# Way back of a Fourier-mix and SoLU kernel: PSUM columns side by side, output tiles by n2 runs, r formed on GpSimd, new schedule keys

## The chip, the cores and the metric

The kernel runs on one core of one Trainium2 chip. The metric is device time in microseconds from launch to end, as the median of several runs. A profiled execution of the same kernel gives the trace that is read below.

## The reference

For each of 8 batches a real Fourier transform along the sequence (3136 positions, 256 channels), a complex 256 x 256 matrix product with bias, a soft threshold, and the inverse transform; then, for each of the 25088 resulting rows, a feed-forward layer with 1024 hidden units, SoLU and a layer norm:

```python
X = np.fft.rfft(x, axis=1)
Yr = Xr @ w_r - Xi @ w_i + b_r
Yi = Xr @ w_i + Xi @ w_r + b_i
Yr = np.sign(Yr) * np.maximum(np.abs(Yr) - lam, 0.0)      # and Yi alike
y = np.fft.irfft(Y, n=3136, axis=1)                       # rows of the second part
h = y @ w_in
e = np.exp(h - h_max)
solu = h * e / (np.sum(e) + 1e-09)
ln = (solu - mu) / np.sqrt(var + 1e-06) * g_ln
out = ln @ w_out
```

All inputs and the output are float32; w_in and w_out come as wide words that the kernel narrows itself.

## The kernel before

The sequence of 3136 is split as 98 x 32 (n1 x n2), so each transform is two small ones. On the way there, `fwd1` transforms along n1 (matmuls with `fq_s` or `fa_s`), `fwd2` along n2 (with `fb`), `mix` multiplies by the weights (`w_hi`, `w_lo`), `threshold` follows on GpSimd, and on the way back `inv1` goes along n2 (with `gb`) and `inv2` along n1 (with `ia_s`, or `iaf_s` in float32 for batch 0). Most factors are split into two f16 parts, high and low, so a product takes three matmuls. Between the steps the data go through DRAM (`s1`, `s2`).

`inv2(b, g)` takes a group of `G2` = 4 values of n2: it loads `zt`, and for each half `eh` of the channels runs 4 x 3 matmuls of 98 columns into one PSUM bank `pv`, seen as (n1, i) with i one of the 4 values of n2. ScalarE then rounds the bank to f16 (`ring_hi`), VectorE forms the rest (`ring_lo`). Of the 98 values of n1 the first 96 go to the rings, the last 2 to `last_hi` and `last_lo`. The rings hold rows of the second part in the order in which they lie there, 128 to a tile.

Each tile of 128 rows goes through three steps. `moe_head`: 12 matmuls of 512 columns with `win_hi`, `win_lo`, `win_low` into a pair of banks, the maximum `m`, some scalars (`ch`, `a`), the exponential on ScalarE and the product `u` on VectorE. `moe_turn`: `lh` (ScalarE) and `ll` (GpSimd), two DMA transposes to `th` and `tl`, the variance `var`, and the scale `r`, in three instructions: a product and sum on VectorE, a power and a product on GpSimd. `moe_tail`: 24 matmuls with `wout`, the scaling by `r` into `o` on ScalarE, and the store of `o`:

```python
out_v = out.rearrange("(b n1 n2) e -> b n1 n2 e", b=B, n1=N1)
n1, n2 = t * P // G2 % N96, t * P // (G2 * N96) * G2
nc.sync.dma_start(out_v[b, n1 : n1 + P // G2, n2 : n2 + G2], o)
```

Every DMA but the first four loads is issued by the one queue of SyncE (SP), in program order. The order of all engines is made at build time by `Plan`: each instruction or group has a key (tables `KEYS`, `SHIFT`, `ROLE`, by stage and role), a cost from `weigh`, and waits; at each point an engine takes the startable operation with the lowest key. All instructions are issued from one line, `issue` (L455, after the change L457), so every row of the profile has that line, and the names of tiles tell the steps apart.

Of the kernel before, what the change touches and what calls it, by code (L numbers as in the profile page):

```python
# [17 lines left out]
AF = mybir.ActivationFunctionType  # L18
ALU = mybir.AluOpType
# [5 lines left out]
S, N1, N2 = 3136, 98, 32  # L25
# [7 lines left out]
S_SCALE, B_SCALE, Z_SCALE, X_SCALE = 2.0**-7, 2.0**-5, 2.0**-11, 2.0**-11  # L33

LOW = 2.0**11
# [209 lines left out]
class Banks:  # L245
# [38 lines left out]


KEYS = {
    "fa": -300, "bias": -182.62, "start": 0, "warm": -200, "plain": -200, "weights": -173.3, "consts": -100,
    "groups": 0, "x0": -51.8, "y0": -216.47, "b0": -80.78, "b0s": 5.87, "w_in0": -120.86, "w_in1": -81.06,
    "w_in": -58.58, "w_out0": -50.76, "w_out": -33.85, "mix": 155.45, "pads": -36.23, "a1": -69.9, "a1s": 8.066,
    "a2": 14.01, "a2s": 1.704, "a": 4.95, "b1": -17.06, "b1s": 1.283, "b": 3.84, "bs": 1.407, "inv2": -93.08,  # L290
    "turn": 239.13, "tail": 4.12, "as": 2.844,
}

SHIFT = {
    "a5": 0.49, "b3": -0.7, "b6": -0.86, "b4": -1.48, "a4": 2.88, "b2": 2.98, "b5": -3.61, "a3": 4.37, "a7": 4.4,
    "a1": -4.81, "a2": -8.16, "a6": -8.71, "b1": 22.31, "b0": -73.49,
}

ROLE = {
    "tail/po": 0.08, "head/u": 0.13, "w_in1/lh": -0.14, "head/ph": -0.28, "tail/o": 0.96, "b/bin": -1.92,  # L300
    "a/bias_y": -2.32, "a/pf": -2.48, "w_out0/lh": 2.64, "w_in1/junk": -2.96, "b/yl": 3.08, "w_out/th": -3.25,
    "b/zs": -3.39, "a/xw0": -3.57, "w_in1/ll": 3.61, "a/un": -4.21, "head/m": -4.36, "inv2/ring_lo": 4.46,
    "w_in1/Du": -5.32, "b/pf": -5.67, "b/Dbin": -5.91, "b/yt": 6.31, "a/hsb": -6.98, "b/y": -8.09,
    "turn/r": -8.25, "b/bin_s16": -8.58, "b/Xh16": -9.67, "w_in0/u": 10.09, "b/Xs": -10.27, "turn/lh": -13.86,
    "a/top": 15.51, "w_out/tl": -15.85, "head/a": 22.29, "tail/Dout": 23.17, "b/Dgb2": 23.89, "a/sc": -25.79,
    "b/zout": -38.98,
}


# [29 lines left out]
class Plan:  # L339
# [68 lines left out]
    def weigh(self, op, name, args, kw, ins, outs):  # L408
        if name == "dma_start":
            v = next(v for v in (*outs, *ins) if not isinstance(v, DramView))  # L410
            size = (v.rows[1] - v.rows[0]) * v.cells.size * mybir.dt.size(v.dtype)
            cross = kw.get("transpose", False)
            op.length += 1600.0 if cross else 430.0
            op.moved += 1500.0 if cross else size / 270.0
        elif op.engine == "tensor":
            moving = ins[-1]
            n = moving.cells.size * (4 if moving.dtype == F32 else 1) * 0.42 + 1
            if moving.cells.size == N1:
                n += 3 * (4 if moving.dtype == F32 else 1)
            lhs = ins[0].tile.kw["name"]  # L420
            op.half = 8 if "gb" in lhs else 4 if lhs == "fq_s" else 2 if moving.tile.kw["name"][:2] == "fb" else 0
            op.length += self.PACE * n / max(op.half, 1)
        else:
            big = max((v.cells.size for v in (*ins, *outs)), default=1)
            scalars = sum(v.cells.size == 1 for v in ins)
            if big == 1:
                scalars -= 2 if name == "tensor_tensor" else 1
            each = self.ELEMENT[op.engine]
            wide = [v for v in ins if v.cells.size > 1]
            sbuf = not any(v.tile.kind.banks for v in (*ins, *outs))  # L430
            if op.engine == "scalar" and sbuf:
                each = 0.87
            if op.engine == "gpsimd" and len(wide) == 2 and all(v.dtype == F32 for v in (*wide, *outs)):
                each = 2.12
            if op.engine == "vector" and sbuf and name in ("tensor_scalar", "tensor_copy") and big > 1:
                each, op.port = 0.545, True
            if op.engine == "vector" and sbuf and len(wide) == 2:
                op.port = True
            if op.engine == "gpsimd":
                op.port = True  # L440
            op.length += self.CALL[op.engine] + big * each + max(scalars, 0) * self.SCALAR[op.engine]
            if "accum_out" in kw and op.engine == "scalar":
                op.length += 92.0
            if ALU.pow in kw.values() or ALU.pow in args:
                op.length += 420.0
# [119 lines left out]
def fft_mix_solu_kernel(ctx: ExitStack, tc, x, w_r, w_i, b_r, b_i, w_in, w_out, g_ln, fa, fq, none, iaf, fb, fs, gb, gs, ia, out):  # L565
    nc = Plan(tc.nc)
    B, _, D = x.shape
    FF = w_in.shape[1]
    P = 128
# [3 lines left out]
    C1 = 1024  # L573
    NCH = N2 * D // C1
    NPK = 8
    out_v = out.rearrange("(b n1 n2) e -> b n1 n2 e", b=B, n1=N1)

    const = Pool(ctx.enter_context(tc.tile_pool(name="const", bufs=1)), 1)
    dram = Pool(ctx.enter_context(tc.tile_pool(name="dram", bufs=2, space=DRAM)), 2, dram=True)
# [4 lines left out]
    banks = Banks(ctx.enter_context(tc.tile_pool(name="ps", bufs=1, space=PSUM)), 8, pf=5, ph=3, po=2, pb=8)  # L584
# [70 lines left out]
    peaks, scales = {}, {}  # L655
# [158 lines left out]
    Xs, Ys = {}, {}  # L814
# [273 lines left out]
    G2 = 4  # L1088
    N96 = N1 - N1 % 16
    R = 2 * G2 * N96  # L1090
    ring_hi = const.tile([P, ND, R], F16, name="ring_hi")
    ring_lo = const.tile([P, ND, R], F16, name="ring_lo")
    lasts = {}

    def inv2(b, g):
        if b >= PLAIN_Z:
            zt = fp.tile([P, G2, 2, D], F16, name="zt", bufs=2)[:N1]
            nc.sync.dma_start(zt.rearrange("c n t d -> c (n t d)"), s2[b][:, g * G2 * 2 * D : (g + 1) * G2 * 2 * D])
        else:
            zt = fp.tile([P, G2, D], F32, name="zt", bufs=2)[:N1]  # L1100
            nc.sync.dma_start(zt.rearrange("c n d -> c (n d)"), s2[b][:, g * G2 * D : (g + 1) * G2 * D])
        j0 = (b * N2 + g * G2) * N96 % R
        if g == 0 and b % 2 == 0:
            lasts[b // 2] = [fp.tile([P, ND, 2, N1 - N96, N2], F16, name=f"last_{part}", bufs=1) for part in ("hi", "lo")]
        for eh in range(ND):
            pv = banks.tile("pf")[:, : G2 * N1].rearrange("p (n i) -> p n i", n=N1)
            to = [
                (
                    ring[:, eh, j0 : j0 + G2 * N96].rearrange("p (n i) -> p n i", n=N96),
                    last[:, eh, b % 2, :, g * G2 : (g + 1) * G2],  # L1110
                )
                for ring, last in zip((ring_hi, ring_lo), lasts[b // 2])
            ]
            nc.reserve(*to[0], *to[1])
            with nc.together():
                for i in range(G2):
                    es = slice(eh * P, (eh + 1) * P)
                    if b < PLAIN_Z:
                        nc.tensor.matmul(pv[:, :, i], zt[:, i, es], iaf_s, start=True, stop=True)
                        continue  # L1120
                    for k, (t, j) in enumerate(((0, 0), (0, 1), (1, 2))):
                        nc.tensor.matmul(pv[:, :, i], zt[:, i, t, es], ia_s[:, j], start=k == 0, stop=k == 2)
            for hi, lo, ns in zip(*to, (slice(0, N96), slice(N96, N1))):
                nc.scalar.activation(hi, pv[:, ns], AF.Copy, scale=X_SCALE)
                nc.vector.scalar_tensor_tensor(lo, hi, -LOW, pv[:, ns], ALU.mult, ALU.add)


    def h_scale(k):
# [48 lines left out]
    def moe_turn(k, u, total, a):  # L1177

        parts = []
        hi = mp.tile([P, FF], F16, name="lh", bufs=2)  # L1180
        nc.scalar.copy(hi, u)
        lo = mp.tile([P, FF], F16, name="ll", bufs=2)
        nc.gpsimd.tensor_sub(lo, u, hi)
        for part, name in ((hi, "th"), (lo, "tl")):
            t = mp.tile([P, NF, P], F16, name=name, bufs=3)
            nc.sync.dma_start(t, part, transpose=True)
            parts.append(t)
        junk = mp.tile([P, FF], BF16, name="junk", bufs=1)
        var = sp.tile([P, 1], F32, name="var")
        nc.scalar.activation(junk, u, AF.Square, bias=total, scale=-float(FF), accum_out=var)  # L1190
        r = sp.tile([P, 1], F32, name="r", bufs=8)
        nc.vector.scalar_tensor_tensor(r, a, a, var, ALU.mult, ALU.add)
        nc.gpsimd.tensor_tensor(r, r, mhalf, op=ALU.pow)
        nc.gpsimd.tensor_tensor(r, r, unscale, op=ALU.mult)
        return k, parts, r

    def moe_tail(k, parts, r):
        th, tl = parts
        po = banks.tile("po")
        n = 0  # L1200
# [6 lines left out]
        o = mp.tile([P, D], F32, name="o", bufs=2)  # L1207
        nc.scalar.activation(o, po[:, :D], AF.Copy, scale=r)
        b, t = k
        if t is None:  # L1210
            for i in range(2):
                nc.sync.dma_start(out[(b + i) * S - P // 2 : (b + i) * S], o[i * P // 2 : (i + 1) * P // 2])
            return
        n1, n2 = t * P // G2 % N96, t * P // (G2 * N96) * G2
        nc.sync.dma_start(out_v[b, n1 : n1 + P // G2, n2 : n2 + G2], o)

# [206 lines left out]
    for b in range(B):  # L1425
# [8 lines left out]
        groups = 0  # L1434
# [36 lines left out]
```

## Time and profile before

| | |
|---|---|
| Median of 3 runs | 1595.03 us (1593.70 to 1598.29) |
| Profiled execution | 1598.61 us, its span 1596.8 us |
| Granted TensorE clock | 0.989 of full speed in the mean |
| Busy share of the span | PE 97%, DVE 83%, ACT 73%, POOL 64% |
| DMA queue of SP | 523596 packets, 268.93 MB, 77.3% of 16 engines' span |

PE is the matmul engine, PEld its weight loads, DVE VectorE, ACT ScalarE, POOL GpSimd, SP the queue that issues DMAs. The span runs from the first to the last instruction. A matmul's duration includes the time in which it overlaps its neighbours, so the distance between starts tells what one costs. A wait is idle time of an engine, put down to what ended it.

### The profile page before, as it was taken

To read this page: it belongs to the slowest core of one execution; us is meant where nothing else is said; L and a number is where in the kernel's file an instruction comes from. 1 tells how busy PE (TensorE), PEld (TensorE's weight loads), DVE (VectorE), ACT (ScalarE), POOL (GpSimd) and SP (SyncE) were. 2 spreads that over 40 slices of the span, in tenths; PEclk is the share of its full clock that TensorE was granted. 3 is DMA by queue.
4 is the path that set the end of the run, shared out by engine and by line. 5 is a ranking of instruction groups with operands and counts; after the bars stand their busy time and mean duration, and the time that the engine had idled before them with its cause. 6 is when DMAs were issued, how large, how long until landed. Compare 5 with 4: busy or idle time off the path is not lost. (4 is left out here: it accounts for less than half of the span.)

```text
span 1596.8 us, 40552 instructions
## 1 busy us (share of the span) xinstructions
PE 1546.1 (97%) x15471; PEld 1090.9 (68%) x15471; DVE 1333.3 (83%) x2767; ACT 1168.7 (73%) x2134; POOL 1017.7 (64%) x1155
## 2 busy tenths in 40 slices
PE   6979999999999999999999999999999999999998
PEld 3435676677666776776776767677776777777776
DVE  5889888978999888888889898888888887777775
ACT  5768777767768877777777767677776877676675
POOL 0646686667766767577764767557765677754554
PEclk8989999999999999999999999999999999999999
DMA  7788768967699598977999789775777965576666
GB/s 251 214 246 181 185 132 183 216 132 164 153 225 198 119 208 181 215 154 167 181 203 214 158 182 204 158 138 121 170 183 166 206 109 130 121 164 139 133 113 123
DMA packets 524239, 273.12 MB, mean 171 GB/s; under 512 B 423680, under 2 KB 501996, under 8 KB 523984
## 3 DMA queue, kind: packets, MB, share of 16 engines
q1 hardware_dynamic: 523596, 268.93, 77.3%
q8 instruction: 121, 1.98, 0.5%
q10 hardware_dynamic: 448, 1.61, 0.3%
q14 instruction: 74, 0.61, 0.1%
HBM read 84.71 MB, written 82.97 MB: 105 GB/s over the span
## 5 line engine op out<-in xcount | busy, mean ns | idle before, releaser
L455 POOL TENSOR_TENSOR ll<-u,lh 128x1024 f16<-128x1024 f32 x196 | 426.3, 2175 | 213.7 <-ACT lh L455 202.2
L455 PE MATMUL store<-wout,th 128*128 128x256 f16 x3136 | 376.6, 273 | 3.7 <-DVE yt L455 2.5
L455 PEld LDWEIGHTS <-th 128*128 128x128 f16 x3136 | 305.9, 99 | 59.2 <-issue 9.7
L455 ACT ACTIVATE u<-store,m,hsb 128x1024 f32<-128x1024 f32 x192 | 231.7, 1207 | 121.7 <-DVE m L455 113.1
L455 DVE TENSOR_REDUCE m<-store 128x1 f32<-128x1024 f32 x196 | 238.9, 1219 | 90.9 <-PE store L455 90.5
L455 PE MATMUL store<-win_hi,ring_hi 128*128 128x512 f16 x768 | 292.6, 381 | 8.1 <-DVE u L455 7.4
L455 PE MATMUL store<-win_lo,ring_hi 128*128 128x512 f16 x768 | 292.3, 381 | 0.0
L455 PE MATMUL store<-win_low,ring_lo 128*128 128x512 f16 x768 | 291.9, 380 | 0.0
L455 ACT CAST lh<-u 128x1024 f16<-128x1024 f32 x196 | 205.6, 1051 | 117.9 <-DVE u L455 69.4
L455 DVE SCALAR_TENSOR_TENSOR u<-store,ch,u 128x1024 f32<-128x1024 f32 x196 | 250.6, 1279 | 40.1 <-ACT u L455 38.4
L455 PEld LDWEIGHTS <-ring_hi 128*128 128x128 f16 x1536 | 149.2, 98 | 154.5 <-issue 17.1
L455 ACT ACTIVATE junk<-u,su 128x1024 bf16<-128x1024 f32 x196 | 226.6, 1156 | 8.3 <-DVE u L455 8.0
L455 PE MATMUL store<-wout,tl 128*128 128x256 f16 x1568 | 203.9, 273 | 0.0
L455 PEld LDWEIGHTS <-tl 128*128 128x128 f16 x1568 | 151.8, 98 | 30.8 <-issue 7.1
L455 PE MATMUL store<-w_hi,Xh 128*128 128x256 f16 (+1 forms) x584 | 166.5, 285 | 6.1 <-ACT Xh L455 3.4
L455 PE MATMUL store<-w_hi,Xl 128*128 128x256 f16 (+1 forms) x584 | 165.9, 284 | 1.4 <-DVE Xl L455 1.1
L455 PE MATMUL store<-w_lo,Xh 128*128 128x256 f16 (+1 forms) x584 | 165.9, 284 | 0.0
L455 DVE SCALAR_TENSOR_TENSOR r<-a,var 128x1 f32<-128x1 f32 x196 | 129.5, 664 | 31.6 <-ACT junk L455 28.3
L455 POOL TENSOR_TENSOR y<-yt,yc 128x512 f32<-128x512 f32 (+1 forms) x104 | 128.1, 1233 | 30.5 <-ACT yt L455 26.2
L455 PEld LDWEIGHTS <-Xh 128*128 128x128 f16 x1168 | 113.8, 99 | 40.7 <-issue 8.9
L455 PEld LDWEIGHTS <-ring_lo 128*128 128x128 f16 x768 | 75.4, 98 | 91.4 <-issue 1.4
L455 POOL TENSOR_TENSOR r<-r,mhalf 128x1 f32<-128x1 f32 x196 | 110.8, 568 | 39.5 <-DVE r L455 26.3
(178 smaller groups left out, 2593.3 us busy)
## 6 DMA issues: line engine op xcount, KB each, us to landing
out_dram<-o SPq DMA_DIRECT2D x192, 128.0 KB
s<-av SPq DMA_DIRECT2D x48, 512.0 KB
zt<-s SPq DMA_DIRECT2D x56, 392.0 KB
s<-zout SPq DMA_DIRECT2D x42, 512.0 KB
xw<-in_x_dram SPq DMA_DIRECT2D x48, 384.0 KB
bin<-s SPq DMA_DIRECT2D x72, 256.0 KB
s1f<-av SPq DMA_DIRECT2D x10, 392.0 KB
xw<-in_x_dram SPq DMA_DIRECT2D x8, 392.0 KB
```

Of the source, the lines that this page charges most:

```text
L455: getattr(engine, name)(*args, **kw)
```

## The change

Four things change. In `inv2` the bank is seen as (i, n1): each matmul writes 98 neighbouring columns, and the rings get rows in the order n2, n1 within a group. A tile of 128 rows is then one to three runs of n1 at fixed n2 (each run of n2 is 96 long), and `moe_tail` stores one run at a time. In `moe_turn` the first of the three instructions for `r` moves from VectorE to GpSimd, as a `tensor_scalar` with two pointers. The tables of keys are new throughout, and `weigh` has a cost for the new GpSimd form.

```diff
 KEYS = {
-    "fa": -300, "bias": -182.62, "start": 0, "warm": -200, "plain": -200, "weights": -173.3, "consts": -100,
+    "fa": -300, "bias": -243.29, "start": 0, "warm": -200, "plain": -200, "weights": -203.16, "consts": -100,
...
+            if op.engine == "gpsimd" and name == "tensor_scalar":
+                each = 1.15
...
-    out_v = out.rearrange("(b n1 n2) e -> b n1 n2 e", b=B, n1=N1)
+    out_v = out.rearrange("(b n1 n2) e -> b n2 n1 e", b=B, n1=N1)
...
-            pv = banks.tile("pf")[:, : G2 * N1].rearrange("p (n i) -> p n i", n=N1)
+            pv = banks.tile("pf")[:, : G2 * N1].rearrange("p (i n) -> p i n", n=N1)
             to = [
                 (
-                    ring[:, eh, j0 : j0 + G2 * N96].rearrange("p (n i) -> p n i", n=N96),
-                    last[:, eh, b % 2, :, g * G2 : (g + 1) * G2],
+                    ring[:, eh, j0 : j0 + G2 * N96].rearrange("p (i n) -> p i n", n=N96),
+                    last[:, eh, b % 2, :, g * G2 : (g + 1) * G2].rearrange("p n i -> p i n"),
...
-                        nc.tensor.matmul(pv[:, :, i], zt[:, i, es], iaf_s, start=True, stop=True)
+                        nc.tensor.matmul(pv[:, i], zt[:, i, es], iaf_s, start=True, stop=True)
...
-                        nc.tensor.matmul(pv[:, :, i], zt[:, i, t, es], ia_s[:, j], start=k == 0, stop=k == 2)
+                        nc.tensor.matmul(pv[:, i], zt[:, i, t, es], ia_s[:, j], start=k == 0, stop=k == 2)
...
-                nc.scalar.activation(hi, pv[:, ns], AF.Copy, scale=X_SCALE)
-                nc.vector.scalar_tensor_tensor(lo, hi, -LOW, pv[:, ns], ALU.mult, ALU.add)
+                nc.scalar.activation(hi, pv[:, :, ns], AF.Copy, scale=X_SCALE)
+                nc.vector.scalar_tensor_tensor(lo, hi, -LOW, pv[:, :, ns], ALU.mult, ALU.add)
...
-        nc.vector.scalar_tensor_tensor(r, a, a, var, ALU.mult, ALU.add)
+        nc.gpsimd.tensor_scalar(r, a, a, var, ALU.mult, ALU.add)
...
-        n1, n2 = t * P // G2 % N96, t * P // (G2 * N96) * G2
-        nc.sync.dma_start(out_v[b, n1 : n1 + P // G2, n2 : n2 + G2], o)
+        p = 0
+        while p < P:
+            n2, n1 = divmod(t * P + p, N96)
+            n = min(N96 - n1, P - p)
+            nc.sync.dma_start(out_v[b, n2, n1 : n1 + n], o[p : p + n])
+            p += n
```

GpSimd's order in the last stretch, before: the power (`r<-r,mhalf`) and the product (`r<-r,unscale`) of one tile's r, then the next tile's `a` and `ll`.

```order
L455 TENSOR_TENSOR ll<-u,lh 128x1024
L455 TENSOR_TENSOR r<-r,mhalf 128x1
L455 TENSOR_SCALAR a<-se,a 128x1
L455 TENSOR_TENSOR r<-r,unscale 128x1
L455 TENSOR_TENSOR ll<-u,lh 128x1024
```

The same place of the change:

```order
L457 TENSOR_TENSOR ll<-u,lh 128x1024
L457 TENSOR_SCALAR r<-a,var 128x1
L457 TENSOR_TENSOR r<-r,mhalf 128x1
L457 TENSOR_SCALAR a<-se,a 128x1
L457 TENSOR_TENSOR r<-r,unscale 128x1
L457 TENSOR_TENSOR ll<-u,lh 128x1024
```

One instruction has come in ahead of the power; VectorE's order has lost its `r<-a,var` rows, 196 in all.

SP's order in the last stretch, before: for each tile two transposes and, between them, the store of an earlier tile.

```order
L455 DMA_TRANSPOSE th<-lh 128x8x128
L455 DMA out_dram<-o 32x4x256
L455 DMA_TRANSPOSE tl<-ll 128x8x128
L455 DMA_TRANSPOSE th<-lh 128x8x128
L455 DMA out_dram<-o 32x4x256
L455 DMA_TRANSPOSE tl<-ll 128x8x128
```

The same place of the change:

```order
L457 DMA_TRANSPOSE th<-lh 128x8x128
L457 DMA out_dram<-o 32x256
L457 DMA out_dram<-o 96x256
L457 DMA_TRANSPOSE tl<-ll 128x8x128
L457 DMA_TRANSPOSE th<-lh 128x8x128
L457 DMA out_dram<-o 96x256
L457 DMA out_dram<-o 32x256
L457 DMA_TRANSPOSE tl<-ll 128x8x128
```

Every store has become two, of 96 and 32 rows or of 64 and 64, between the same transposes; 200 stores of `o` have become 392.

PE's order at the very start, before (the `fa_s` matmuls are the first transform of batch 0, the `yc` matmuls spread the biases, the `u,ones` ones sum the weights):

```order
L455 MATMUL store<-ones 128x128 x12
L455 MATMUL store<-xw_86,fa_s 98x512 x2
L455 MATMUL store<-u,fa_s 98x512 x2
L455 MATMUL store<-xw_86,fa_s 98x512 x2
L455 MATMUL store<-u,fa_s 98x512 x4
L455 MATMUL store<-xw_100,fa_s 98x512 x2
L455 MATMUL store<-u,fa_s 98x512 x2
L455 MATMUL store<-xw_100,fa_s 98x512 x2
L455 MATMUL store<-yc,ones 128x512
L455 MATMUL store<-yc,yt 128x256 x2
L455 MATMUL store<-u,ones 128x256 x4
```

The same place of the change:

```order
L457 MATMUL store<-ones 128x128 x12
L457 MATMUL store<-xw_86,fa_s 98x512 x2
L457 MATMUL store<-yc,ones 128x512
L457 MATMUL store<-yc,yt 128x256 x2
L457 MATMUL store<-u,fa_s 98x512 x4
L457 MATMUL store<-xw_86,fa_s 98x512 x2
L457 MATMUL store<-u,fa_s 98x512 x2
L457 MATMUL store<-xw_101,fa_s 98x512 x2
L457 MATMUL store<-u,fa_s 98x512 x2
L457 MATMUL store<-xw_101,fa_s 98x512 x2
L457 MATMUL store<-u,ones 128x256 x4
```

The bias matmuls have moved ahead of most of the first transform; PE has 29863 rows in both orders.

## Rows read from the trace of the kernel before

**Rows 1.** The page, busy time, share of the span and instructions of each engine.

```profile
PE 1546.1 (97%) x15471; PEld 1090.9 (68%) x15471; DVE 1333.3 (83%) x2767; ACT 1168.7 (73%) x2134; POOL 1017.7 (64%) x1155
```

**Rows 2.** Busy time by stretch: length, each engine, granted clock, DMA share, GB/s.

```profile
0.00:100.00 100.00, 80.72 (x837) 39.82 (x837) 75.09 (x142) 70.77 (x135) 40.77 (x40) 0.93 0.77 235
...
300.00:1500.00 1200.00, 1186.22 (x12149) 856.15 (x12148) 1018.00 (x2115) 887.10 (x1624) 793.48 (x906) 1.00 0.79 168
```

**Rows 3.** The chain that ended last: start, length, what.

```profile
1213.37 379.10 PE store L455 x3467
```

**Rows 4.** PE's waits: total us, times, longest us (first two, last of 20).

```profile
PE store L455 <- DVE u L455: 7.9, 9, 2.2
PE store L455 <- ACT bin L455: 6.9, 1, 6.9
...
PE store L455 <- POOL Xl L455: 0.2, 1, 0.2
```

**Rows 5.** PE in order of time, 1300 to 1310 us: start, length, what.

```profile
1300.16 1.57 PE L455 MATMUL store<-fb,bin 64*128 64x64 f16 x96
1301.67 1.05 PE L455 MATMUL store<-wout,tl 128*128 128x256 f16 x8
1302.55 0.38 PE L455 MATMUL store<-win_hi,ring_hi 128*128 128x512 f16 x1
...
1305.14 2.19 PE L455 MATMUL store<-ia_s,zt 98*128 98x98 f16 x24
1307.12 1.95 PE L455 MATMUL store<-wout,th 128*128 128x256 f16 x16
1308.91 1.04 PE L455 MATMUL store<-wout,tl 128*128 128x256 f16 x8
1309.79 0.27 PE L455 MATMUL store<-w_hi,Xh 128*128 128x256 f16 x1
```

**Rows 6.** Groups of PE by form: count, busy us, mean ns, idle before.

```profile
L455 PE MATMUL store<-ia_s,zt 98*128 98x98 f16 x1344 | 122.2, 286 | 1.6 <-ACT o L455 0.9 <-DVE yt L455 0.6
...
L455 PE MATMUL store<-iaf_s,zt 98*128 98x98 f32 x128 | 15.3, 274 | 0.0
```

**Rows 7.** PE in order of time, at 111 and at 456 us.

```profile
111.14 3.71 PE L455 MATMUL store<-iaf_s,zt 98*128 98x98 f32 x32
114.68 0.38 PE L455 MATMUL store<-win_hi,ring_hi 128*128 128x512 f16 x1
...
456.25 0.40 PE L455 MATMUL store<-fs_s,bin_s 128*128 128x128 f16 x4
456.48 0.71 PE L455 MATMUL store<-wout,th 128*128 128x256 f16 x5
```

**Rows 8.** Groups of ACT by form.

```profile
L455 ACT ACTIVATE ring_hi<-store 128x384 f16<-128x384 f32 x128 | 62.1, 495 | 40.5 <-PE store L455 40.1
...
L455 ACT ACTIVATE Xh<-store 128x512 f16<-128x512 f32 x104 | 57.2, 603 | 19.3 <-DVE Xs L455 13.9 <-PE store L455 5.1
```

**Rows 9.** Groups of DVE and of POOL by form.

```profile
L455 DVE SCALAR_TENSOR_TENSOR r<-a,var 128x1 f32<-128x1 f32 x196 | 129.5, 664 | 31.6 <-ACT junk L455 28.3 <-POOL r L455 1.1 <-POOL yc L455 1.0
...
L455 POOL TENSOR_SCALAR yc<-yt,sc 128x512 f32<-128x512 f32 x84 | 68.6, 817 | 56.6 <-DVE yt L455 40.0 <-DVE ch L455 15.2 <-DVE a L455 1.1
L455 POOL TENSOR_SCALAR a<-se,a 128x1 f32<-128x1 f32 x196 | 56.1, 286 | 95.9 <-ACT u L455 37.2 <-DVE a L455 33.5 <-PE store L455 2.1
```

**Rows 10.** SP's issues in order of time, 1502 to 1556 us.

```profile
1502.17 1.24 SPq L455 DMA_TRANSPOSE th<-lh  x1
1503.65 0.56 SPq L455 DMA_DIRECT2D out_dram<-o  x1
1504.31 1.27 SPq L455 DMA_TRANSPOSE tl<-ll  x1
...
1555.12 1.23 SPq L455 DMA_TRANSPOSE th<-lh  x1
```

**Rows 11.** Busy time by stretch, columns as in rows 2.

```profile
640.00:680.00 40.00, 40.00 (x384) 28.53 (x382) 34.82 (x92) 30.65 (x57) 20.68 (x29) 1.00 1.07 209
```

More of the change, by code (lines that the diff above doesn't have):

```diff
@@ L286 @@
 KEYS = {
-    "fa": -300, "bias": -182.62, "start": 0, "warm": -200, "plain": -200, "weights": -173.3, "consts": -100,
[L288 to L291, printed above, removed]
+    "fa": -300, "bias": -243.29, "start": 0, "warm": -200, "plain": -200, "weights": -203.16, "consts": -100,
@@ L292 @@
+    "groups": 0, "x0": -175.82, "y0": -51.96, "b0": -115.32, "b0s": 4.277, "w_in0": -161.15, "w_in1": -112.71,
+    "w_in": -109.53, "w_out0": -71.07, "w_out": -17.01, "mix": 116.28, "pads": -69.29, "a1": -75.67,
+    "a1s": 10.825, "a2": 18.06, "a2s": 1.034, "a": 0.49, "b1": -21.98, "b1s": 1.959, "b": 2.06, "bs": 1.538,
+    "inv2": -85.41, "turn": 153.65, "tail": 3.96, "as": 1.842,
 }
 SHIFT = {
-    "a5": 0.49, "b3": -0.7, "b6": -0.86, "b4": -1.48, "a4": 2.88, "b2": 2.98, "b5": -3.61, "a3": 4.37, "a7": 4.4,
@@ L296 @@
-    "a1": -4.81, "a2": -8.16, "a6": -8.71, "b1": 22.31, "b0": -73.49,
+    "b4": -0.33, "b6": 1.62, "a5": 2.05, "b5": -2.17, "b2": 2.33, "a4": 2.62, "b3": -3.91, "a6": -6.82,
+    "a7": -10.33, "a2": -10.77, "a3": 12.99, "b1": 20.66, "b0": -70.35,
 }
 ROLE = {
-    "tail/po": 0.08, "head/u": 0.13, "w_in1/lh": -0.14, "head/ph": -0.28, "tail/o": 0.96, "b/bin": -1.92,
-    "a/bias_y": -2.32, "a/pf": -2.48, "w_out0/lh": 2.64, "w_in1/junk": -2.96, "b/yl": 3.08, "w_out/th": -3.25,
-    "b/zs": -3.39, "a/xw0": -3.57, "w_in1/ll": 3.61, "a/un": -4.21, "head/m": -4.36, "inv2/ring_lo": 4.46,
@@ L303 @@
[L303 to L306, printed above, removed]
+    "head/ph": -0.29, "w_in1/u": 0.37, "b/bin": 0.51, "a/both": 0.58, "head/u": -0.59, "b/Xl": 0.68,
+    "a/av": 0.68, "a/peaks": 1.29, "b/yl": 1.86, "b/Dgb2": 1.92, "w_in0/u": 2.5, "inv2/last_hi": -3.37,
@@ L307 @@
+    "a/hsb": 3.92, "weights/u": 3.99, "a/v": 4.16, "a/un": 4.33, "a/pf": -5.05, "head/m": 5.41,
+    "w_out0/lh": 5.94, "b/pf": -6.04, "b/Xh16": -6.25, "w_in0/Du": -6.43, "b/yt": 6.86, "a/xw1": -7.25,
+    "turn/junk": 7.47, "b/Xs": -7.58, "inv2/last_lo": -8.25, "b/Dgb3": 8.73, "b/y": -10.12, "b/zs": 10.35,
+    "w_in1/ll": 10.7, "w_out/o": 12.33, "b/bin_s16": -13.08, "w_out/wout": 17.67, "turn/ll": 24.16,
+    "head/a": 36.36, "a/sc": -39.48, "b/zout": -44.76,
 }
```

## The prediction

> **What bounds the kernel now.** I read the page's busy line first: TensorE (PE) is busy for 1546.1 us of a 1596.8 us span, VectorE (DVE) for 83%, ScalarE (ACT) for 73%, GpSimd (POOL) for 64% [rows 1]. [...] The chain that ended last is PE work without a break for its last 379.1 us, 3467 matmuls [rows 3]. The view of PE's waits has 20 rows that add up to 46.1 us; the longest single one, 6.9 us on ACT's `bin`, falls in the first 100 us, as do 19 us in all, so some 27 us lie after it [rows 2, 4]. So the kernel runs at PE's rate almost everywhere: what shortens a PE instruction stream shortens the kernel, and what other engines gain or lose counts only where PE comes to wait for it.
>
> Because matmuls overlap, I take the cost of one from the distance between starts, not from its duration. In a late stretch [rows 5] twelve matmuls of 512 columns start between 1302.55 and 1305.14 us: 216 ns each. Eight of 256 columns take from 1308.91 to 1309.79: 110 ns. That is 0.414 ns a column and about 4 ns beside it. The 24 matmuls of one `inv2` group, 98 columns each, take from 1305.14 to 1307.12: 82.5 ns each, where a straight line through the two others gives 110 - 158 x 0.414 = 44.6 ns. They pay twice the column time (2 x 98 x 0.414 = 81). What sets them apart in the code is that each writes every fourth fp32 of its PSUM bank (`pv[:, :, i]`).
>
> **The change part by part.** *Columns side by side.* `inv2` now writes 98 neighbouring words (`pv[:, i]`). The trace has 1344 such f16 matmuls in 56 groups [rows 6]. If the step in PSUM is what doubles them, each falls from 82.5 to 44.6 ns: 1344 x 37.9 = 50.9 us off PE. The bounds: nothing, if something else makes them slow; and a spacing of (456.48 - 456.25) / 4 = 57.5 ns, that of the `fs_s` matmuls, which also load weights of their own for each 128 columns [rows 7], worth 1344 x 25 = 33.6 us. I take 50.9, because 57.5 is just what 128 columns cost on the line above, so that row shows no floor of its own, and because the `fb` matmuls, each with its own weights, follow each other at 1.51 us / 96 = 15.7 ns [rows 5]. The 128 fp32 records of batch 0 (`iaf_s`) start (114.68 - 111.14) / 32 = 110.6 ns apart [rows 6, 7]; whether they gain nothing or the same 37.9 ns (4.9 us in all) no row says: I take 2 us.
>
> The trace shows here that a stepped output doubles a matmul of 98 columns, or is at least found with it [rows 5]. [...]
>
> *Evictions.* ACT and DVE now read PSUM in four runs of 96 with a step instead of one run of 384. No row shows such a read; the nearest is `Xh`, written in 16 runs of 32, at 603 ns for 512 elements against 495 for `ring_hi`'s 384 [rows 8], the same 0.84 ns an element between them, so runs cost nothing there. Even 50 ns more on each of 128 would be 6 us on an ACT that is idle for 27% of the span: nothing on the path.
>
> *r on POOL.* DVE loses 196 instructions of 664 ns in the mean, 129.5 us, for one element a partition [rows 9]; other DVE work behind them starts earlier. PE's waits on DVE outside the first 100 us add up to some 18 of the 46.1 us, the longest of them 7.9 us on `u` [rows 4]; I take 3 us of gain, bounds 0 and 9. POOL gets 196 more: at least 286 ns each (`a`, the same operation with one pointer), at most 817 ns (`yc`, two pointers and 512 elements) [rows 9], so 56 to 160 us; near the `a` row since the size is that of `a`, some 70 us. POOL then stands at (1017.7 + 70) / 1545 = 70%. Behind r on POOL's queue stand its power, its product and the next tile's `ll`; ACT's `lh` and SP's transposes wait for `ll`. PE's list has no wait on a transpose at all, so this has room, and I cost it at nothing; if that cover were gone, each tile would lose the 0.36 us of its r.
>
> *Two stores a tile.* Runs of 96 rows cut into tiles of 128 always give two pieces, so 192 stores become 384, on SP's one queue. A store of 128 rows takes 0.56 us to issue [rows 10], whatever its rows as far as the trace can say; so up to 192 x 0.56 = 107.5 us more on SP. In the last stretch SP spends 1.24 + 0.56 + 1.27 = 3.07 us on a tile that takes (1555.12 - 1502.17) / 9 = 5.88 us [rows 10]; after, 3.63 of some 5.6 us. It is hidden as long as SP has slack; behind the second store on SP stands the next tile's transpose, and PE's order has three to four other heads between a tile's head and its tail, some 20 us of work. The rows of a piece lie 32 KiB apart in DRAM where four used to lie together; each is still 1 KiB, and with a DMA share of 1.07 PE still was busy for 40.00 of 40 us [rows 11]. I cost both at nothing, and the risk below.
>
> *New keys.* They move work by a few us everywhere; the excerpts show it at PE's start, where the two bias matmul groups run early. The stream of PE has as many instructions as before. A faster PE also asks the other engines and the DMAs for 3% more in the same time. For both I put 5 us of new waits; bounds -3 and +27 (the waits after the first 100 us, doubled).
>
> **Sum.** The profiled execution took 1598.6 us: 1598.6 - 50.9 - 2 - 3 + 5 = 1547.7. It was 3.6 us above the median of the three runs, 1595.0, so the forecast for the median is 1544 us, 3.2% less.
>
> **The rivals.** *The weights set the pace.* Each `inv2` matmul loads 128 columns of weights of its own, and 82.5 ns could be the time of a load and a matmul in turn. Then PSUM's layout gives nothing and the time is 1595 - 3 + 5 = 1597; with a floor of 57.5 ns it is 1595.0 - 33.6 = 1561 before the small terms. Against it stand the 57.5 and 15.7 ns of the two rows above, with weights of their own, and that the excess is one column time exactly. [...] Chance 0.10, split between 1597 and 1561.
>
> *The gain is given back in waits.* The path would leave PE in the stretches where the fronts of later batches run beside the tiles and DVE was busiest. If the 27 us of waits after the first 100 us double, or the new order misses a transfer in a few places, 20 to 30 us come back: 1564 to 1574. For it: the keys are new everywhere, and the DMA share was above 1 in some stretches. Against it: DVE falls to (1333 - 129) / 1545 = 78%, and the lead of heads over tails is the same in both orders. Chance 0.10.
>
> *SP becomes the bound (slower).* The second store stands in front of the next transpose on SP; if SP never has slack, each of 192 costs its 0.56 us in full: 1544 + 107 = 1651. It turns slower than before once more than half of that shows. The point from which it decides is where SP's work on a tile exceeds PE's, 5.6 us; in the late stretch it is 3.63, and loads of the fronts would have to add 2 us a tile. Chance 0.05.
>
> **How the numbers follow.** Forecast 0.75, the weights 0.10, waits 0.10, SP 0.05. A change under 0.3% (5 us) can't be told from none here. Faster by more: 0.75, most of the waits (0.09) and half of the weights (0.05), 0.89. Same: the other half of the weights, 0.05. Slower: SP and a remainder, 0.06. Range: the low end takes every bound that helps, 50.9 + 4.9 + 9 off 1595, 1531; the high end the 57.5 ns floor with 15 us of new waits, 1577.
>
> **What would show it.** Right: a group of 24 `ia_s` matmuls lasting about 1.1 us from its start to the next group's, not 1.98; PE's busy time near 1495 us with its share still 96 to 97%; no `r<-a,var` on DVE and one of some 0.3 to 0.4 us on POOL; 392 store issues, SP waiting less on PE. Wrong, and how: the groups still at 1.98 us (the step was not the cause); the groups at 1.1 us but PE idle for 70 us or more (its waits then name the engine); SP's rows back to back with PE waiting for transposes (the stores).

## The result and the profile after

The change takes the median from 1594.97 us (1593.70 to 1598.29) to 1537.85 us (1535.26 to 1542.55, four runs): a ratio of 0.9642 with a 95% interval of 0.9612 to 0.9672. The profiled execution took 1535.88 us, its span 1533.9 us. The forecast was 1544, with a range of 1531 to 1577.

The page of the changed kernel, busy time, share of the span and instructions of each engine:

```profile
PE 1489.9 (97%) x15471; PEld 1036.4 (68%) x15471; DVE 1226.8 (80%) x2571; ACT 1166.3 (76%) x2134; POOL 1084.9 (71%) x1351
```

PE's busy time has fallen by 56.2 us against [rows 1], the span by 62.9; the difference between the two, PE's idle time, went from 50.7 to 44.0 us. PE is still busy 97% of the span. DVE has lost 196 instructions and 106.5 us, POOL has gained 196 and 67.2 us.

Busy time by stretch, columns as in [rows 2]:

```profile
0.00:100.00 100.00, 82.56 (x835) 40.40 (x836) 70.93 (x136) 68.15 (x130) 39.99 (x40) 0.91 0.77 228
300.00:1440.00 1140.00, 1129.62 (x12089) 801.47 (x12082) 929.47 (x1949) 882.51 (x1619) 847.35 (x1060) 1.00 0.85 176
```

PE is idle for 10.4 us in 1140, a little less than the 14 in 1200 of before [rows 2], though ACT, POOL and the DMAs (0.85 of their time, 0.79 before) now have more to do in a microsecond; DVE has less. The idle time of the first 100 us is 17.4 us, 19.3 before. Runs that keep the old order there have 16.4 to 19.4 us, so no effect of the new order of the bias matmuls can be seen.

PE's waits, total us, times and longest, the first four of 24 rows:

```profile
PE store L457 <- DVE top L457: 6.6, 1, 6.6
PE store L457 <- ACT bin L457: 6.5, 1, 6.5
PE store L457 <- DVE Xl L457: 4.0, 5, 1.5
PE store L457 <- DVE u L457: 3.9, 5, 1.5
```

The wait that stood first in [rows 4], on DVE's `u`, has halved, from 7.9 to 3.9 us. Groups by form, of PE, ACT and POOL, to be read against [rows 6, 8, 9]:

```profile
L457 PE MATMUL store<-ia_s,zt 98*128 98x98 f16 x1344 | 69.4, 206 | 1.2 <-DVE Xl L457 1.0 <-DVE zout L457 0.2
L457 PE MATMUL store<-iaf_s,zt 98*128 98x98 f32 x128 | 15.3, 273 | 0.0
L457 ACT ACTIVATE ring_hi<-store 128x384 f16<-128x384 f32 x128 | 61.7, 499 | 4.9 <-DVE ch L457 3.6 <-DVE last_lo L457 1.3
L457 POOL TENSOR_SCALAR r<-a,var 128x1 f32<-128x1 f32 x196 | 74.8, 383 | 36.4 <-ACT junk L457 32.2 <-DVE bin L457 1.1
```

The `ia_s` group is busy for 52.8 us less than in [rows 6]. The fp32 group hasn't moved, and the rounding that now reads PSUM in four runs of 96 takes 499 ns where it took 495 [rows 8]. POOL's new instruction takes 383 ns.

The fp32 matmuls in order of time, and SP's queue in a late stretch (start, length, what):

```profile
114.26 3.71 PE L457 MATMUL store<-iaf_s,zt 98*128 98x98 f32 x32
117.81 0.38 PE L457 MATMUL store<-win_hi,ring_hi 128*128 128x512 f16 x1
```

```profile
1447.86 1.23 SPq L457 DMA_TRANSPOSE th<-lh  x1
1449.53 1.14 SPq L457 DMA_DIRECT2D out_dram<-o  x2
1450.77 1.27 SPq L457 DMA_TRANSPOSE tl<-ll  x1
1453.06 1.24 SPq L457 DMA_TRANSPOSE th<-lh  x1
1454.54 0.85 SPq L457 DMA_DIRECT2D out_dram<-o  x2
```

The fp32 spacing is (117.81 - 114.26) / 32 = 110.9 ns, 110.6 before [rows 7]. It is that of the records: the code has 64 fp32 matmuls there, so each stands as two of the 128. Two stores take SP 0.85 to 1.14 us where one took 0.56 [rows 10]. A tile then holds SP for 1.23 + 1.14 + 1.27 = 3.64 us of the 1453.06 - 1447.86 = 5.20 us between two `th`.

### The profile page after: what moved, and what is told of

The parts are those of the page before. It is cut to its first block, busy times and chain, and to the rows that moved or that the text cites. A ratio compares the mean times of both kernels' runs of the same rounds, so it can differ in the third digit from the quotient of the medians.

```text
span 1533.9 us, 40789 instructions
## 1 busy us (share of the span) xinstructions
PE 1489.9 (97%) x15471; PEld 1036.4 (68%) x15471; DVE 1226.8 (80%) x2571; ACT 1166.3 (76%) x2134; POOL 1084.9 (71%) x1351
## 4 chain that ended last, share of the span: by engine, by line
PE 51%; DVE 3%; ACT 1%; issue 1%; POOL 1%; DMA 1%; SPq 0%; DVEq 0%; ACTq 0%; POOLq 0%
PE store L457 51%; DMA xw<-in_x_dram 1%; POOL ll L457 1%; DVE m L457 1%; DVE u L457 0%; ACT u L457 0%; ACT lh L457 0%; DVE bin L457 0%; DVE peaks L457 0%; DMA th<-lh 0%; SPq L457 0%; DVE yt L457 0%; DVE xw L457 0%; POOL r L457 0%; ACT junk L457 0%
## 5 line engine op out<-in xcount | busy, mean ns | idle before, releaser
L457 POOL TENSOR_TENSOR yl<-y,yh 128x512 f16<-128x512 f32 x96 | 112.8, 1179 | 18.5 <-ACT yh L457 18.1
L457 ACT ACTIVATE o<-store,r 128x256 f32<-128x256 f32 x196 | 93.3, 477 | 40.3 <-PE store L457 36.9
```

The costliest lines, as they stand in the source:

```text
L457: getattr(engine, name)(*args, **kw)
```

## The experiments

Twelve kernels were run. The first four asked which part brings the gain. The next four kept each engine's order as it was, so that the engine of `r` could be seen by itself. The last four asked what in the step costs, and tried two boundaries.

**Contiguous writes alone.** The kernel before, one line:

```diff
-            pv = banks.tile("pf")[:, : G2 * N1].rearrange("p (n i) -> p n i", n=N1)
+            pv = banks.tile("pf")[:, : G2 * N1].rearrange("p (i n) -> p n i", n=N1)
```

> The kernel before, with the PSUM columns side by side and nothing else: each matmul of inv2 writes 98 neighbouring words, and the evictions read the bank with a step of 98 words so that the rings, the tiles, the stores, the keys and the order of every engine stay those of before. If the step of the write is the cause, the ia_s matmuls follow each other at 46 ns instead of 82 to 84 and about 52 us leave PE: 1540 to 1548 us. If the gain came from the new order, the time is above 1580 us, and PE's gaps show where the 50 us went. If weight loads set the pace, the spacing stays above 80 ns and the time at 1595. The stepped reads may make ring_hi and ring_lo slower than 495 and 545 ns; up to 600 ns each this is hidden.

Measured: 1566.85 us (1560.36 to 1569.38), ratio 0.9809 [0.9785, 0.9833]. The page, the group, DVE's `r` and the longest wait of DVE and of PE:

```profile
PE 1495.9 (96%) x15471; PEld 1037.8 (67%) x15471; DVE 1339.6 (86%) x2767; ACT 1161.8 (75%) x2134; POOL 1016.8 (65%) x1155
```

```profile
L455 PE MATMUL store<-ia_s,zt 98*128 98x98 f16 x1344 | 70.3, 206 | 6.1 <-ACT o L455 3.0 <-DVE yt L455 2.1 <-DVE Xl L455 0.9
L455 DVE SCALAR_TENSOR_TENSOR r<-a,var 128x1 f32<-128x1 f32 x196 | 145.0, 743 | 60.5 <-ACT junk L455 55.9 <-POOL yc L455 2.3 <-POOL r L455 1.1
```

```profile
DVE r L455 <- ACT junk L455: 55.9, 64, 2.7
```

```profile
PE store L455 <- DVE u L455: 10.2, 10, 2.2
```

The group has given up the same 52 us (122.2 to 70.3), but by the medians only 28 of them reach the end: neither the 47 to 55 that were expected of the step nor none. (In the profiled executions 38 do; this one is the fastest of five that spread over 9 us.) DVE now stands 55.9 us in front of `r` until ACT's `junk` is done (28.3 in [rows 9]), and its 196 records take 145.0 us in place of 129.5. PE's idle time is 1558.5 - 1495.9 = 62.6 us, 12 more than before.

**r on POOL alone, planned anew.** The kernel before, with the old keys:

```diff
-        nc.vector.scalar_tensor_tensor(r, a, a, var, ALU.mult, ALU.add)
+        nc.gpsimd.tensor_scalar(r, a, a, var, ALU.mult, ALU.add)
...
+            if op.engine == "gpsimd" and name == "tensor_scalar":
+                each = 1.15
```

> The kernel before, with r's first instruction on POOL and its cost entered in the planner, nothing else. VectorE's 130 us for r were off the path, so the forecast is 1592 to 1595 us: at most 3 us of PE's waits go. The rival that VectorE's relief made part of the 57 us says 1585 or less.

Measured: 1607.88 us (1605.73 to 1612.40), ratio 1.0078 [1.0058, 1.0098]: 0.8% slower, by neither expectation. The planner moved much else with it, so by itself this run doesn't tell what the engine of `r` is worth.

**The step back.** The changed kernel, order unchanged:

```diff
-            pv = banks.tile("pf")[:, : G2 * N1].rearrange("p (i n) -> p i n", n=N1)
+            pv = banks.tile("pf")[:, : G2 * N1].rearrange("p (n i) -> p i n", n=N1)
```

> The changed kernel with the stepped PSUM writes put back (the bank as n1, i; evictions read it with a step of 4), the order of every engine as in the change. If the step is the cause: 1537.9 + 52 = 1590 us, with ia_s spacing 82 to 84 ns. If order, stores and r make the gain, it stays below 1560.

Measured: 1584.33 us (1583.88 to 1590.69), ratio 0.9936 [0.9914, 0.9958]. The step is worth 46.5 us here, near the 52 of the expectation, against 28 in the kernel before: the rest of the change lets more of it through.

**r back on DVE, planned anew.** The changed kernel with the line of `r` of before.

> The changed kernel with r's first instruction back on VectorE and planned so. Forecast: within 5 us of the change, 1538 to 1543 us, since VectorE then stands at 87% of a shorter span; the rival that VectorE becomes the next limit once PE is faster says 1550 or more, with PE's waits naming VectorE.

Measured: 1592.57 us (1588.20 to 1600.19), ratio 0.9979 [0.9963, 0.9994], 55 us more than the changed kernel: the rival of that expectation. PE's longest wait:

```profile
PE store L457 <- DVE u L457: 14.1, 18, 2.5
```

Either `r` on DVE costs 55 us, or the plan that the planner makes around it does. The next two separate these, since in them `r` is planned on one engine and issued on the other.

**r issued on DVE in the changed kernel's own order.**

```diff
...
+                    if op.role == "r" and name == "tensor_scalar":
+                        self.nc.vector.scalar_tensor_tensor(*args, **kw)
+                        continue
```

> The changed kernel with the order of every engine kept as it is, except that r's 196 records, still planned as POOL's, are issued on DVE at their place in the plan. Theory: with the matmuls at 46 ns DVE with r (145.8 us of records in the run with r back on DVE) is the next limit, so taking r off it is what lets the rest of the 53 us through: near 1592 like that run, 1565 to 1595. Rival: in that run it was the new plan around r and not r's engine that cost 55 us: then this one, whose order is the changed kernel's own, stays near 1538 to 1545. The spacing of the ia_s matmuls is 46 ns by both.

Measured: 1560.95 us (1556.82 to 1561.63), ratio 0.9777 [0.9758, 0.9797]: between the two expectations. So some 23 us of the 55 are the engine's, and 32 are the other plan's. DVE's `r` here and PE's two longest waits:

```profile
L458 DVE SCALAR_TENSOR_TENSOR r<-a,var 128x1 f32<-128x1 f32 x196 | 89.0, 456 | 7.2 <-ACT junk L460 5.9 <-POOL a L460 0.8 <-issue 0.3
```

```profile
PE store L460 <- DVE u L460: 10.7, 11, 2.4
PE store L460 <- DVE Xl L460: 7.0, 7, 2.1
```

At the places that were chosen for POOL, DVE hardly waits for `junk`, and its records are shorter; it is still late with `u` and `Xl` more often than in the changed kernel (3.9 and 4.0 us).

**Contiguous writes and r issued on POOL, all else as before.** The first diff above, and

```diff
...
+                    if op.role == "r" and name == "scalar_tensor_tensor":
+                        self.nc.gpsimd.tensor_scalar(*args, **kw)
+                        continue
```

> The kernel before with PSUM written side by side, its old keys, its one store for a tile and its order of every engine, except that r, planned as DVE's, is issued on POOL at its place. Theory (r's engine decides once the matmuls are faster): about 1567 - 29 = 1538, 1535 to 1545, with DVE near 80% busy. Rival (the new keys and their plan decide): near 1567, or slower, since r on POOL alone in an unsuited plan gave 1608 against 1595 (13 us more): 1565 to 1580.

Measured: 1538.49 us (1537.12 to 1539.85), ratio 0.9637 [0.9617, 0.9656], as the theory had it. With the old keys, the old order and one store a tile this is the time of the changed kernel, 0.9642 [0.9612, 0.9672]. New keys, the rows' order and the second store together are thus worth nothing that these runs can tell.

**r issued on POOL alone, order as before.** The second diff above without the first.

> The kernel before in its own order, with r issued on POOL at its place and nothing else changed: the cell that is missing beside before, contiguous writes alone (1567) and both (1538). Theory: with the ia_s matmuls at 84 ns PE's own work is the bound and DVE (145 us of r or none) has slack, so this changes nothing: 1590 to 1597. Rival: r's engine is worth some 28 us whatever the matmuls take: 1565 to 1570, and it is the terms that add, not one that uncovers the other.

Measured: 1585.40 us (1580.89 to 1586.31), ratio 0.9928 [0.9915, 0.9942]. Neither expectation: it gains 10 us, not none and not 28. The four cells, each beside the 1595 to 1597 us that the kernel before took in the same session:

| | r on DVE | r on POOL |
|---|---|---|
| stepped writes | 1 | 0.9928, 9.8 us less |
| contiguous writes | 0.9809, 28.3 us less | 0.9637, 58.5 us less |

Alone the two are worth 38 us; together 58. Each uncovers 20 us of the other. The changed kernel with the step put back, 1584.33 us, agrees with the upper right cell, 1585.40: there too the new keys, the rows' order and the second store show no effect.

**r on DVE without its wait.** Contiguous writes alone, with `a` read in place of `var`:

```diff
...
+                    if op.role == "r" and name == "scalar_tensor_tensor":
+                        args[3] = args[1]
```

> Contiguous writes alone, order unchanged, with r left on DVE but reading a a third time in place of var (so the output's scale is another): DVE still issues r's 196 records, and doesn't wait for ACT's junk. Theory A (r costs because DVE, which works in order, stands still until junk is done, 55.9 us of idle time in the run with contiguous writes alone): near 1538 to 1545. Theory B (r costs because its records themselves are long on DVE, a mean of 743 ns): 1560 to 1570, with r's records as long as before. In between, both.

Measured: 1553.45 us (1552.00 to 1554.56), ratio 0.9734 [0.9722, 0.9747]: in between. DVE's `r`, and a wait of POOL:

```profile
L457 DVE SCALAR_TENSOR_TENSOR r<-a 128x1 f32<-128x1 f32 x196 | 168.6, 864 | 1.2 <-POOL a L457 1.0
```

```profile
POOL r L457 <- DVE r L457: 20.5, 15, 3.9
```

The wait is gone (60.5 to 1.2 us) and 13 of the 28 us with it. The other 15 are still lost while `r` is on DVE; its records have grown from 743 to 864 ns in the mean, and POOL still waits 20.5 us for them before its power. Which of these two carries how much of the 15 was not separated. What makes a record of one element a partition so long is seen in order of time. DVE and POOL in the run with contiguous writes alone (start, length, what):

```profile
1051.14 1.87 DVE L455 SCALAR_TENSOR_TENSOR r<-a,var 128x1 f32<-128x1 f32 x1
1052.93 0.14 DVE L455 TENSOR_SCALAR ch<-m 128x1 uint32<-128x1 uint32 x1
...
1055.82 0.74 DVE L455 SCALAR_TENSOR_TENSOR yt<-store,un,bias_y 128x512 f32<-128x512 f32 x1
1056.48 0.21 DVE L455 TENSOR_SCALAR m<-m,hsb 128x1 f32<-128x1 f32 x1
...
1057.40 0.68 DVE L455 SCALAR_TENSOR_TENSOR r<-a,var 128x1 f32<-128x1 f32 x1
```

```profile
1050.86 2.12 POOL L455 TENSOR_TENSOR ll<-u,lh 128x1024 f16<-128x1024 f32 x1
...
1055.92 2.14 POOL L455 TENSOR_TENSOR ll<-u,lh 128x1024 f16<-128x1024 f32 x1 [0.67 <-ACT lh L455]
```

Both `r` begin inside an `ll` and end with it: 1051.14 + 1.87 = 1053.01 and 1050.86 + 2.12 = 1052.98; 1057.40 + 0.68 = 1058.08 and 1055.92 + 2.14 = 1058.06. Inside the second `ll`, DVE's `m`, with one tensor input, takes 0.21 us; `yt`, with an input in PSUM, begins just before it and takes 0.74; neither lasts until the `ll` ends. The whole trace of the kernel before says the same. 96 of the 196 `r` begin inside an `ll`; none ends before it, and 89 end 13 to 21 ns after it. The 27 during which POOL does nothing take 198 to 222 ns. `m<-m,hsb` takes 206 ns in the median inside an `ll` and 205 outside. So the length of an `r` on DVE is mostly not work, but the rest of an `ll` (or of a like operation of POOL), and what follows on DVE starts only as it ends (`ch` at 1052.93 behind the first `r`): at some 0.21 us each the 196 would take 41 us, so by this estimate 104 of the 145.0 us are waiting. `r` has `a` and `var` as inputs, and in the run without the wait `a` twice; why it lasts as long as the `ll` was not shown. On POOL the same product takes 383 ns and doesn't run beside an `ll`: in POOL's own order it stands behind one.

**What in the step costs: pairs, and every second word.** The kernel before, twice, with other places for a result's columns in the bank, so that the evictions read them in permuted order (`bank` is the part of the bank that `pv` views; the `iaf_s` line changes in the same way). First pairs, then every second word:

```diff
+            pm = bank.rearrange("p (m i t) -> p i m t", i=G2, t=2)
...
-                        nc.tensor.matmul(pv[:, :, i], zt[:, i, t, es], ia_s[:, j], start=k == 0, stop=k == 2)
+                        nc.tensor.matmul(pm[:, i], zt[:, i, t, es], ia_s[:, j], start=k == 0, stop=k == 2)
```

> The kernel before with the ia_s and iaf_s matmuls writing two neighbouring words and then skipping six, so that a result of 98 columns lies as 49 pairs; the result's columns land in permuted places, order and evictions are those of before. [...] Rival (any step in the row costs): spacing 84 ns and about 1595.

```diff
+            pm = bank.rearrange("p (h n j) -> p h n j", h=2, j=2)
...
-                        nc.tensor.matmul(pv[:, :, i], zt[:, i, t, es], ia_s[:, j], start=k == 0, stop=k == 2)
+                        nc.tensor.matmul(pm[:, i // 2, :, i % 2], zt[:, i, t, es], ia_s[:, j], start=k == 0, stop=k == 2)
```

> The kernel before with the ia_s and iaf_s matmuls writing every second word in place of every fourth; the result's columns land in permuted places, order and evictions are those of before. Theory (one word in each pair, whatever the distance): spacing 84 ns and about 1595. Rival (the price goes with the distance): between 46 and 84 ns, near 59 for a third of the way, and 1570 to 1585.

One run each: 1562.8 us for pairs, near the 1566.85 of contiguous writes alone and not the 1595 of the rival, and 1596.28 us for every second word, as its theory had it. The `ia_s` group of the first, then of the second:

```profile
L455 PE MATMUL store<-ia_s,zt 98*128 98x98 f16 x1344 | 70.4, 206 | 6.0 <-ACT o L455 2.7 <-DVE yt L455 2.3 <-DVE Xl L455 0.9
```

```profile
L455 PE MATMUL store<-ia_s,zt 98*128 98x98 f16 x1344 | 122.2, 286 | 1.6 <-ACT o L455 0.9 <-DVE yt L455 0.6
```

Pairs that are six words apart cost what contiguous columns cost: their group is busy for 70.4 us, against 70.3 with contiguous writes alone. Single words cost more, and at a distance of two the same as at four: 122.2 us in both. Why pairs are spared was not shown.

**Batch 0 in f16 too.** The changed kernel with

```diff
-    PLAIN, PLAIN_Z = 2, 1
+    PLAIN, PLAIN_Z = 2, 0
```

> The changed kernel with the way back of batch 0 in f16 like that of the other batches: 128 iaf_s records at 112 ns go, 384 of ia_s at 45 ns come, which is 14.3 - 17.3 = 3 us more of PE by the spacings, and 128 records' worth of splitting comes to DVE, ACT or POOL. Expected 1535 to 1550. Rival: the fp32 weights' loads or the wait at that stage are what costs, and the time falls by 3 to 6 us.

Measured: 1572.77 us (1566.85 to 1575.34), ratio 0.9851 [0.9833, 0.9869]: 35 us slower than the changed kernel, and worse than either expectation. Its plan is another one. The `ia_s` group and PE's two longest waits, of which the changed kernel has the first at 3.9 us and the second not among its first four:

```profile
L457 PE MATMUL store<-ia_s,zt 98*128 98x98 f16 x1536 | 82.7, 210 | 16.4 <-DMA zt<-s 9.5 <-DVE yt L457 4.3 <-DVE u L457 2.4
```

```profile
PE store L457 <- DVE u L457: 19.4, 13, 5.2
PE store L457 <- DMA zt<-s: 9.5, 3, 7.7
```

The expectation had miscounted: 1536 - 1344 = 192 matmuls come, not 384, since 128 fp32 records are 64 matmuls. By the spacings that is 192 x 45 - 128 x 111 ns, some 5.6 us less of PE instead of 3 more. How much of the 35 us is the f16 path and how much the plan was not separated.

**Eight stores a tile.** The kernel before, order unchanged:

```diff
-        nc.sync.dma_start(out_v[b, n1 : n1 + P // G2, n2 : n2 + G2], o)
...
+        with nc.together():
+            for i in range(8):
+                c = P // G2 // 8
+                nc.sync.dma_start(out_v[b, n1 + i * c : n1 + (i + 1) * c, n2 : n2 + G2], o[i * P // 8 : (i + 1) * P // 8])
...
```

The lines left out enter an eighth of the old cost for each store, so that the plan stays.

> The kernel before with each output tile stored in eight pieces in place of one, order unchanged. By my step on the stores (SP issues at 0.32 to 0.56 us each, hidden while SP waits for PE): some 2.5 us of transposes and 8 x 0.43 = 3.4 us of stores is 5.9 us a tile on SP against 5.9 of PE, so about the point where SP decides: 1595 to 1640, with SP's waits on PE nearly gone. Rival: pieces of 16 rows issue faster than 0.43 us and nothing changes: 1590 to 1600.

Measured: 2093.89 us (2086.44 to 2097.17), ratio 1.3115 [1.3091, 1.3139]. SP in order of time, its wait for PE (here, then in the kernel before, then in the changed kernel with two stores a tile), PE's longest wait, and PE's busy time from the page:

```profile
1509.33 1.23 SPq L456 DMA_TRANSPOSE th<-lh  x1
1510.65 5.39 SPq L456 DMA_DIRECT2D out_dram<-o  x8
1516.16 1.25 SPq L456 DMA_TRANSPOSE tl<-ll  x1
```

```profile
SPq L456 <- PE store L456: 48.6, 49, 7.8
```

```profile
SPq L455 <- PE store L455: 350.1, 199, 7.8
```

```profile
SPq L457 <- PE store L457: 230.9, 152, 7.5
```

```profile
PE store L456 <- DMA tl<-ll: 90.8, 35, 10.8
```

```profile
PE 1686.4 (81%) x15471; PEld 1147.1 (55%) x15471; DVE 1310.9 (63%) x2767; ACT 1171.3 (56%) x2134; POOL 1018.3 (49%) x1155
```

Eight stores hold SP for 5.39 us, 0.67 each, and with two transposes a tile takes SP 7.9 us where PE needs 5.9 [rows 10]. SP hardly waits for PE any more, and PE waits for transposes. The sign was expected, the size was not: I had taken 0.43 us a store from the pairs above, and pieces of 16 rows take half as much again. Two us more on each of 196 tiles are some 390 of the 499 us. The rest was not separated: SP also issues the loads and stores of the fronts, which the expectation had left out, and PE's own busy time grew by 140 us against [rows 1], at a granted clock of 0.905 in the mean where it was 0.989.

## Why the prediction was right

**The step in PSUM.** Predicted 82.5 to 44.6 ns, 50.9 us off PE. The changed kernel has 48 such matmuls from 1213.69 us to the next group at 1215.85:

```profile
1213.69 2.32 PE L457 MATMUL store<-ia_s,zt 98*128 98x98 f16 x48
1215.85 1.04 PE L457 MATMUL store<-wout,tl 128*128 128x256 f16 x8
```

That is 45.0 ns, so 1344 x 37.5 = 50.4 us. The mechanism and the size hold: contiguous writes alone, in an unchanged order, bring the group down, and the two runs on pairs and single words show what in the step costs. The floor of 57.5 ns, kept as a rival, doesn't appear, though every one of these matmuls loads weights of its own.

**What of it reaches the end.** I put the whole 50.9 us on the path, because PE was idle so little, and beside it 3 us (0 to 9) for `r` off DVE, as if each had its price by itself. Beside `r` on POOL the step is worth what I said, or nearly: 46.5 us when it is put back in the changed kernel. Without that it is worth 28.3, and what is missing is what `r` then holds back: from contiguous writes alone to both it is 1566.85 - 1538.49 = 28.4 us. So the term of `r` is the mis-sized one: 9.8 us by itself, just over its upper bound, and 28.4 behind the step that the sum had already taken (in the profiled executions 21.6). Taken the other way round, `r` brings 9.8 us and the step behind it 46.9. Either way the two bring some 57 us, where the sum had 50.9 + 3. That the sum came so near is in part luck: it priced the step as if `r` were already off DVE, and the change happened to take it off. With `r` left on DVE the same reasoning was 19 us or more too low (1540 to 1548 expected, 1566.85 measured). I had read the price of `r` from PE's waits on DVE in the trace of before, and there a slower PE hides a late DVE. What could have shown it stood in [rows 9]: 28.3 us of DVE's time in front of `r`, and a mean of 664 ns for one element a partition, which I took for work. The time of contiguous writes alone lies in the range of my rival of gains given back (1564 to 1574), though with the old keys; that it didn't decide here is due to `r`.

**New waits.** Predicted 5 us (-3 to 27). PE's idle time fell by 6.7 us in the profiled executions, which holds the gain from `r` as well; no wait took the place of the old ones.

**fp32 matmuls.** Predicted 2 us (0 to 4.9): nothing, the spacing is 110.9 ns as before; why the step costs fp32 nothing is open. **Evictions** cost 4 ns each, as good as nothing. **r on POOL** was put at some 70 us and 70% of POOL, with 0.3 to 0.4 us an instruction: 74.8 us, 71% and 383 ns. DVE, put at 78%, stands at 80%. **Two stores** were costed at nothing, which holds: with one store the time is the same, and SP's wait for PE has only shrunk, from 350.1 to 230.9 us. A tile of 128 rows is always two runs, never one or three. The rival in which SP decides is real, at another number of stores.

**New keys.** Worth nothing with `r` on POOL. But when the planner plans anew for `r` on the other engine with the keys left as they are, the time is 22 to 32 us above that of the old plan with `r` merely issued there (1607.88 against 1585.40 us, and 1592.57 against 1560.95).

**The range.** By its own terms its low end is 1595 - 64.8 = 1530 us, not 1531; nothing hangs on it.

## What to carry to other kernels

Where one engine is 97% busy, the waits of its trace price the other engines only at the pace it has now: ask again for each edit what the second engine will be late with once the first is faster, and look at small instructions whose mean is several times their shortest. Where a planner orders the work, try an edit with the order held fixed as well, because a new plan moved this kernel by more than some of the edits did.

## What the runs showed of the hardware

An `r` on VectorE, one element a partition with two tensor inputs, lasted until the end of a GpSimd operation on two wide tensors that was running when it began. In the kernel before 115 of the 196 began in one (`ll`, `y`, `yl`, `Xl`), and none ended before it. Of the 12 that began in a `yc`, which has one wide tensor, three ended some 0.5 us before it. In the run without the wait all 196 took between 197 and 2143 ns (shortest, median, longest):

```profile
L457 DVE SCALAR_TENSOR_TENSOR r<-a x196: 197/684/2143, 140.9 to 1537.9; 128x1 f32<-128x1 f32 x196
```

At a granted clock of 1.00, matmuls of 98 f16 columns, each with its own weights, followed each other at 45.0 ns with the columns side by side (the changed kernel at 1213.69 us), and at 82.5 ns as single words at a step of four [rows 5]. The group of 1344 was busy for 70.4 us in pairs and 70.3 side by side, and for 122.2 us at a step of two as of four. In fp32 each is two records, 110.6 ns apart with the step and 110.9 without it, at 1.00 too. A store of 16 rows held SP longer (0.67 us) than one of the two that share a tile (0.43 to 0.57), and why is open.
